# Sparse attention and a gated expert layer: the largest of v by TensorE, stores from ScalarE, a fifth softmax buffer, the gate's product kept in PSUM, the threshold on ScalarE

## The chip, the core and the metric

The kernel runs on one core of one Trainium2 chip. The metric is the device time of one execution in microseconds, the lower the better. One execution of the kernel before was also profiled: its trace gives start, length and engine of each instruction, and who released whom. The engines are TensorE (PE, with its weight loads shown as PEld), VectorE (DVE), ScalarE (ACT), GpSimd (POOL) and SyncE (SP, which before the change issues all DMAs).

## What is computed

Eight batches of eight heads, 576 queries and keys, 64 columns a head; then a layer of 512 to 2048 to 512 over the 4608 rows.

```python
scores = (1/8) * q @ k.T
thresh = scores.max(-1) - tau                 # tau = 0.02
attn = exp(where(scores >= thresh, scores, -1e9) - max)
attn = attn / (attn.sum(-1) + 1e-9)
x = concat_heads(attn @ v)                    # 4608 x 512
h = x @ w_in                                  # 4608 x 2048
out = (h * sigmoid(h)) @ w_out                # 4608 x 512
```

## The kernel before

Everything is held to nearly float32 precision by splitting operands into a high and a low float16 part, so that a product is three matmuls (high by high, high by low, low by high). The parts need a common scale, a power of two from the largest magnitude.

**Attention.** A *tile* is 128 queries of one head against all 576 keys; there are 288 tiles, and 36 for each batch from the second on (batch 0 is worked on in two rounds, whose first is in plain float32). The numbers in tile names count slots, some of which are empty, so that the last is 300. A tile goes through the engines like this: PE writes the scores into one of two PSUM buffers (L406); DVE takes the negated maximum (L416) and from it the threshold, maximum minus tau (L419, a 128x1 operation); ACT takes exp of the scores into an SBUF buffer w32 (L426), of which there are four in turn; DVE zeroes what is below the threshold and sums the rest (L435), which frees the scores' PSUM buffer, and takes the sum's reciprocal (L439, L443); ACT scales w32 (L448); POOL writes the high part (L459) and the two pieces of the low part (L462, L465) into a buffer hl, and with that last read w32 is free again; SP issues the DMA that transposes hl into wT (L475). When a pair of heads is complete, PE multiplies wT with the parts of v (L490), and ACT and DVE split the result into the high and the low part of x (L508, L509).

**v.** For each batch the four pieces of v are loaded (L227), DVE takes the largest magnitude of each in every partition (L233) and of the four (L110), and POOL's custom instruction partition_all_reduce takes the largest over the partitions (L113). Six small DVE operations make scales of it (L116 to L131), and then ACT and DVE split v (L270, L271).

**Experts.** A group of 256, 320 or 288 columns is worked on in units: 16 units of h, one for each 128 rows of d_ff, with 12 matmuls (L524), then 16 quarters of o with 12 matmuls each (L562), four to each output block. h and o take the same PSUM banks in turn: three (m0 to m2) from the middle of batch 0 on, two before that. After a unit of h come four operations: ACT takes tanh of h/2 into a buffer th in SBUF, of which there are two (L532); DVE makes (tanh + 1) * h and writes it back into th (L533), the last read of the bank; ACT writes its high part, times 2^-14, into gbuf (L541; the first four of the run are written by POOL, L543); DVE writes the low part (L547). After the fourth quarter of o, ACT scales the bank into one of two buffers ot (L571) and SP issues the store (L573).

**Order.** Python emits all this slot by slot, one tile and some units of the experts in each, with a pace that spreads the units of a group over the tiles until the next one; a scheduler then orders the instructions of each engine by priority and by its own idea of time, and adds the waits. Each engine, and SP's queue of DMAs, runs its instructions strictly in that order. When attention is done, the experts of the last groups are left. The two decoders of the weights at the start (L173 to L206) share the engines with batch 0.

Of the kernel before, what the change touches and what calls it, by code (L numbers as in the profile page):

```python
# [28 lines left out]
GB = 17  # buffers of g: a group of 16 and one ahead  # L29
WSPARE = 2  # raw weights lie this far ahead of the split ones, which take their place  # L30
LOAD = 5  # tiles that the loads of q and k run ahead
AV_LAG = 3  # tiles from a visit's last to its product with v
EARLY = 36  # tiles in which ACT still rounds the weights of attention for GpSimd
GAP, GAP1 = 12, 1  # free slots before batch 0's second visits and before batch 1
V_SLOT = 26  # batch 0's values are split from here on
RATES = (1.3, 0.8)  # units of the experts per slot while batch 0's two groups are there
RATE = 0.95
# weights: first chunk, slots of the decoding and of the splitting, priority
# [3 lines left out]
# a visit of two heads: its tiles of 128 queries (4: the last 64 of both heads) for the  # L42
# first and the second head, and the query ranges that it completes
# [8 lines left out]
def attention_moe(  # L52
# [21 lines left out]
    # three banks in turn; the last one is for the sums of the weights while they come in  # L74
# [7 lines left out]
    # ---------------------------------------------------------------- constants  # L82
    tau_sb = const.tile([P, 1], F32, name="tau_sb")
    nc.sync.dma_start(out=tau_sb, in_=tau)
    # 1/8 where the threshold can be met (tau >= 0), else 0: all scores equal, all kept
# [9 lines left out]
    # stacks of (hi; lo) rows of q, with 64 zero columns for the shared tile  # L95
# [9 lines left out]
    def pow2_scales(mx, name, across=True):  # L105
        """From mx [P, n] (bounds >= 0, per partition or, without across, the same on all):
        s = 2^(13-e) and 1/s for the largest's exponent e."""
# [3 lines left out]
        if across:  # L111
            allp = const.tile([P, 1], F32, name=f"{name}_all", tag=f"{k}_all")
            nc.gpsimd.partition_all_reduce(allp, one, P, bass.bass_isa.ReduceOp.max)  # L113
            one = allp
# [21 lines left out]
    # ---------------------------------------------------------------- weights  # L136
# [29 lines left out]
    def decode_weights(i):  # L166
        """float64 words to float32: the sign, 8 bits of the exponent (2^-112 on the top word
        read as float32 takes the exponent's bias down), 23 of the fraction."""
# [15 lines left out]
        # sums of the magnitudes over the rows of four chunks, four columns at a time: they  # L184
        # bound h (w_in), w_out
# [33 lines left out]
    # ---------------------------------------------------------------- values  # L219
# [56 lines left out]
    # ---------------------------------------------------------------- q and k  # L276
# [12 lines left out]
    def qcol(h, i):  # L289
        """Column of query tile i in the stack (even: 0..3, last, zeros; odd: zeros, last,  # L290
        2, 3, 0, 1)."""
        return i * P if h % 2 == 0 else (0, 384, 512, 128, 256)[(i + 1) % 5]
# [30 lines left out]
    # the first visits work in float32 throughout: the tensor engine has time for them  # L323
# [53 lines left out]
    # ---------------------------------------------------------------- scores  # L377
    # a tile: (visit, [(head, query tile, first row, rows)])
# [32 lines left out]
    def soft1(t):  # L411
        s_ps = sps[t]
        sm = sb.tile([P, 5], F32, tag="small", name=f"sm_{t}", bufs=4)
        w = sb.tile([P, S], F32, tag="w32", name=f"w32_{t}", bufs=4)
        negm, thr = sm[:, 0:1], sm[:, 1:2]
        nc.vector.tensor_reduce(  # L416
            out=negm, in_=s_ps[:, :, :HALF], op=ALU.max, axis=AX.XY, negate=True
        )
        nc.vector.tensor_scalar(  # L419
# [5 lines left out]
    def soft1b(t):  # L425
        nc.scalar.activation(  # L426
            wtile[t].rearrange("p (j c) -> p j c", j=2), sps[t][:, :, :HALF], AF.Exp,
            bias=small[t][:, 0:1],
        )
# [351 lines left out]
```

## Time and profile before

| | |
|---|---|
| runs | median 1358.73 us, 1357.87 to 1359.26 (3 runs) |
| profiled execution, span from its first to its last instruction | 1360.4 us |
| last instruction of POOL's work on attention | about 1236 us |
| mean granted clock of PE over the span | 0.950 |
| stores: size and time from issue to landing | 56 of 144 KB, 2.0 us |
| transposing DMAs (L475) | 304, 3.3 us |
| instructions that load a table of functions on ACT | 1, of 1.3 us |

The span of the profiled execution is what the profile has for its own time; it lies 1.7 us above the median of the runs. Rows of groups read: line, engine, operation, result<-operands, partitions x elements, count | busy us, mean ns of one | idle time of the engine before them, and what ended most of it. In a timeline the brackets at the end of a row give that idle time and its releaser for one instruction; "issue" stands for a wait that the profile does not explain. Rows of waits read: who waited <- for whom: us in total, times, longest.

### The profile page before, as it was taken

What the parts mean: (1) busy time and instruction counts of PE and PEld (TensorE: products, weight loads), DVE (VectorE), ACT (ScalarE), POOL (GpSimd) and SP (SyncE); (2) the same over time, 40 slices, a digit from 0 to 9 for tenths busy, and PEclk for the clock granted to TensorE, in tenths of its full rate; (3) what the DMA queues carried; (4) which work ended last, traced back from release to release, by engine and by line L of the source; (5) the groups of instructions that cost most, each with busy time, mean ns of one, the idle gap of its engine ahead of it and who ended that gap; (6) DMA issues with size and microseconds to landing.
All of it is one profiled execution on the core that took longest, in us unless ns stands there. A gap on an engine that the chain in (4) does not pass through costs nothing.

```text
span 1360.4 us, 26858 instructions
## 1 busy us (share of the span) xinstructions
PE 1183.7 (87%) x9392; PEld 899.9 (66%) x9392; DVE 1002.8 (74%) x2619; ACT 817.5 (60%) x1493; POOL 789.9 (58%) x964
## 2 busy tenths in 40 slices
PE   3774787898599979898899969899799999999998
PEld 2453555666477757676677757677577777777777
DVE  4987997897598967968497856869478787872421
ACT  3776775675476756656375745757367666662432
POOL 2647984787478656754476646556467666661000
PEclk9887888999799999999899979999799999999999
DMA  6454955778467656664475556565466565543000
GB/s 226 140 185 125 197 129 94 146 139 170 88 133 155 122 106 129 131 128 86 99 132 124 118 96 136 101 127 121 82 122 116 115 129 115 106 88 53 6 19 18
DMA packets 363479, 158.15 MB, mean 116 GB/s; under 512 B 329552, under 2 KB 338256, under 8 KB 363344
## 3 DMA queue, kind: packets, MB, share of 16 engines
q1 hardware_dynamic: 363344, 156.43, 55.5%
q8 instruction: 74, 1.21, 0.4%
q14 instruction: 61, 0.50, 0.1%
HBM read 66.72 MB, written 9.44 MB: 56 GB/s over the span
## 4 chain that ended last, share of the span: by engine, by line
DVE 35%; PE 34%; issue 13%; ACT 6%; POOL 6%; DMA 5%; SPq 2%; POOLq 0%; ACTq 0%; DVEq 0%
PE o L562 15%; PE h L524 8%; DVE w L435 8%; DVE sm L416 6%; DVE gbuf L547 6%; PE s L406 5%; PE a L490 5%; DVE qstack L310 3%; DVE th L533 3%; DMA vraw<-in_vL 2%; DMA wT<-hl 2%; ACT w L426 2%; POOL hl L459 2%; POOL hl L462 2%; ACT w L448 2%
## 5 line engine op out<-in xcount | busy, mean ns | idle before, releaser
L524 PE MATMUL h<-x,wst 128*128 128x288 f16 (+2 forms) x3072 | 422.3, 290 | 22.6 <-DVE th L533 19.1
L562 PE MATMUL o<-gbuf,wst 128*128 128x288 f16 (+2 forms) x3072 | 419.4, 293 | 22.4 <-DVE gbuf L547 16.1
L562 PEld LDWEIGHTS <-wst 128*128 128x128 f16 x3072 | 296.4, 100 | 117.1 <-issue 27.1
L459 POOL TENSOR_SCALAR hl<-w 128x576 f16<-128x576 f32 x264 | 187.3, 710 | 317.9 <-ACT w L448 69.1
L524 PEld LDWEIGHTS <-wst 128*128 128x128 f16 x3072 | 290.7, 99 | 119.2 <-issue 37.5
L462 POOL TENSOR_TENSOR hl<-w,hl 128x512 f16<-128x512 f32 x272 | 332.0, 1220 | 28.0 <-issue 13.9
L426 ACT ACTIVATE w<-s,sm 128x576 f32<-128x576 f32 x288 | 211.0, 736 | 204.5 <-POOL hl L465 135.4
L435 DVE SCALAR_TENSOR_TENSOR w<-s,sm,w 128x576 f32<-128x576 f32 x288 | 232.6, 810 | 110.4 <-ACT w L426 108.7
L448 ACT ACTIVATE w<-w,sm 128x576 f32<-128x576 f32 x288 | 218.2, 770 | 86.5 <-DVE sm L443 81.6
L416 DVE TENSOR_REDUCE sm<-s 128x1 f32<-128x576 f32 x288 | 215.1, 748 | 44.4 <-PE s L406 42.3
L406 PE MATMUL s<-khi,qstack 128*128 128x288 f32 x608 | 160.4, 346 | 70.0 <-DVE w L435 36.9
L547 DVE SCALAR_TENSOR_TENSOR gbuf<-th,gbuf 128x288 f16<-128x288 f32 (+2 forms) x256 | 167.3, 656 | 20.9 <-ACT gbuf L541 20.2
L406 PEld LDWEIGHTS s<-khi,qstack 128*128 128x128 f32 x608 | 98.5, 198 | 98.8 <-issue 71.4
L490 PE MATMUL a<-wT,v 128*64 128x288 f16 (+1 forms) x1680 | 142.4, 294 | 16.1 <-DMA wT<-hl 15.0
L532 ACT ACTIVATE th<-h,msc 128x288 f32<-128x288 f32 (+2 forms) x256 | 126.3, 495 | 49.5 <-DVE gbuf L547 30.0
L541 ACT ACTIVATE gbuf<-th 128x288 f16<-128x288 f32 (+2 forms) x252 | 109.9, 438 | 44.5 <-DVE th L533 43.9
L406 PE MATMUL s<-klo,qstack 128*128 128x288 f32 x608 | 134.2, 304 | 0.0
L533 DVE SCALAR_TENSOR_TENSOR th<-th,h 128x288 f32<-128x288 f32 (+2 forms) x256 | 113.2, 444 | 27.6 <-ACT th L532 25.4
L490 PEld LDWEIGHTS <-v 128*64 128x64 f16 x1680 | 91.3, 110 | 56.7 <-issue 41.9
L465 POOL TENSOR_TENSOR hl<-w,hl 128x64 f16<-128x64 f32 x272 | 115.3, 424 | 0.0
L406 PEld LDWEIGHTS s<-klo,qstack 128*128 128x128 f32 x608 | 102.2, 197 | 0.0
L320 POOL TENSOR_TENSOR klo<-kraw,khi 128x576 fp32r<-128x576 f32 x64 | 95.6, 1493 | 1.4 <-ACT khi L318 1.3
(82 smaller groups left out, 868.8 us busy)
## 6 DMA issues: line engine op xcount, KB each, us to landing
qraw<-in_qT SPq DMA_DIRECT2D x128, 144.0 KB, 3.0
kraw<-in_kT SPq DMA_DIRECT2D x128, 144.0 KB, 3.0
vraw<-in_vL SPq DMA_DIRECT2D x32, 320.0 KB, 3.5
wraw<-in_w_out SPq DMA_DIRECT2D x16, 512.0 KB, 4.0
out_t<-ot SPq DMA_DIRECT2D x56, 144.0 KB, 2.0
wT<-hl SPq DMA_TRANSPOSE x304, 3.3
gbuf<-in_w_in SPq DMA_DIRECT2D x8, 512.0 KB, 5.1
wraw<-in_w_in SPq DMA_DIRECT2D x8, 512.0 KB, 4.9
```

What stands on the lines that cost most here:

```text
L406: nc.tensor.matmul(s_ps[:, j, :HALF], lhs, kk[:, j * HALF : (j + 1) * HALF], start=(n == 0), stop=(n == len(seq) - 1),)
L416: nc.vector.tensor_reduce(out=negm, in_=s_ps[:, :, :HALF], op=ALU.max, axis=AX.XY, negate=True)
L426: nc.scalar.activation(wtile[t].rearrange("p (j c) -> p j c", j=2), sps[t][:, :, :HALF], AF.Exp, bias=small[t][:, 0:1],)
L435: nc.vector.scalar_tensor_tensor(out=w3, in0=s_ps[:, :, :HALF], scalar=sm[:, 1:2], in1=w3, op0=ALU.is_ge, op1=ALU.mult, accum_out=sm[:, 2:3],)
L448: nc.scalar.activation(w, w, AF.Copy, scale=r)
L459: nc.gpsimd.tensor_scalar(out=fl[:, 0:S], in0=w, scalar1=1.0, scalar2=1.0, op0=ALU.mult, op1=ALU.mult)
L462: nc.gpsimd.tensor_tensor(out=fl[:, 640:1152], in0=w[:, 0:512], in1=fl[:, 0:512], op=ALU.subtract)
L490: nc.tensor.matmul(a_ps[odd * D : (odd + 1) * D, :n], vt[:, lo_v, odd, kv, :], wT[v, b * H + 2 * p + odd][:, kw, c0 - base : c0 - base + n ...
L524: nc.tensor.matmul(ph[:, :n], wi(c, f, lo_w), x16[b, lo_x][:, c, c0 : c0 + n], start=(k == 0), stop=(k == 11),)
L533: nc.vector.scalar_tensor_tensor(out=th[:, :n], in0=th[:, :n], scalar=1.0, in1=ph[:, :n], op0=ALU.add, op1=ALU.mult,)
L547: nc.vector.scalar_tensor_tensor(out=g[:, 1, :n], in0=th[:, :n], scalar=2.0**-14, in1=g[:, 0, :n], op0=ALU.mult, op1=ALU.subtract,)
L562: nc.tensor.matmul(ps[:, :n], wo(f, d, lo_w), g[:, lo_g, :n], start=(f == 0 and k == 0), stop=(f == NF - 1 and k == 2),)
```

## The change

- **Largest of v.** L113 is gone. ACT scales the rows of the 128x128 identity by the per-partition maxima, in bfloat16 (new L115), PE multiplies a matrix of ones with this diagonal (L117), so that each partition holds all 128 maxima in one PSUM bank of the rotation, and DVE takes their maximum (L119).
- **Threshold.** L419 is gone from DVE; ACT computes it after exp as -1 * negm + ntau (L432).
- **Softmax buffers.** Five of w32 instead of four.
- **Gate.** (tanh + 1) * h is written back into the PSUM bank of h instead of th (L538, before L533); the high part (L545, now always ACT) and the low part (L546, before L547) read it there.
- **Stores.** The result o is scaled into two spare places of the weights' array instead of buffers of its own, and its store is issued by ACT instead of SP (L573).
- Comments are gone, which moves the line numbers by some lines: L406 is L411, L416 is L421, L426 is L428, L435 is L440, L448 is L453, L459, L462, L465 are L464, L467, L470, L524 is L529, L562 is L561.

```diff
         if across:
-            allp = const.tile([P, 1], F32, name=f"{name}_all", tag=f"{k}_all")
-            nc.gpsimd.partition_all_reduce(allp, one, P, bass.bass_isa.ReduceOp.max)
-            one = allp
+            diag = const.tile([P, P], BF16, name=f"{name}_diag", tag="diag")
+            nc.scalar.activation(diag, ident, AF.Copy, scale=one)
+            allp = bank([P, P], f"{name}_ps")
+            nc.tensor.matmul(allp, ones, diag, start=True, stop=True)
+            one = const.tile([P, 1], F32, name=f"{name}_all", tag=f"{k}_all")
+            nc.vector.tensor_reduce(out=one, in_=allp, op=ALU.max, axis=AX.X)
...
-        w = sb.tile([P, S], F32, tag="w32", name=f"w32_{t}", bufs=4)
+        w = sb.tile([P, S], F32, tag="w32", name=f"w32_{t}", bufs=5)
...
-        nc.vector.tensor_scalar(
-            out=thr, in0=negm, scalar1=-1.0, scalar2=ntau, op0=ALU.mult, op1=ALU.add
-        )
...
+        nc.scalar.activation(
+            small[t][:, 1:2], small[t][:, 0:1], AF.Identity, scale=-1.0, bias=ntau
+        )
...
             nc.vector.scalar_tensor_tensor(
-                out=th[:, :n], in0=th[:, :n], scalar=1.0, in1=ph[:, :n],
+                out=ph[:, :n], in0=th[:, :n], scalar=1.0, in1=ph[:, :n],
...
-            if gcount[0] > 4:
-                nc.scalar.activation(g[:, 0, :n], th[:, :n], AF.Copy, scale=2.0**-14)
-            else:
-                nc.gpsimd.tensor_scalar(
-                    out=g[:, 0, :n], in0=th[:, :n], scalar1=2.0**-14, scalar2=1.0,
-                    op0=ALU.mult, op1=ALU.mult,
-                )
+            nc.scalar.activation(g[:, 0, :n], ph[:, :n], AF.Copy, scale=2.0**-14)
             nc.vector.scalar_tensor_tensor(
-                out=g[:, 1, :n], in0=th[:, :n], scalar=2.0**-14, in1=g[:, 0, :n],
+                out=g[:, 1, :n], in0=ph[:, :n], scalar=2.0**-14, in1=g[:, 0, :n],
...
-            o = sb.tile([P, WID], F32, tag="o", name=f"ot_{b}_{c0}_{d}", bufs=2)
+            o = wst[:, NW + d % 2, :]
...
-            nc.sync.dma_start(out=outT[d * P : (d + 1) * P, c : c + n], in_=o[:, :n])
+            nc.scalar.dma_start(out=outT[d * P : (d + 1) * P, c : c + n], in_=o[:, :n])
```

The scheduler orders each engine anew. Three places show how.

POOL, before, at the all-reduce for batch 4, while it splits the weights of tiles 121 and 122 (ISA rows are custom instructions or what sets them up):

```order
L459 TENSOR_SCALAR hl_121_5756<-w32_121_5715 128x576
L462 TENSOR_TENSOR hl_121_5756<-w32_121_5715,hl_121_5756 128x512
L465 TENSOR_TENSOR hl_121_5756<-w32_121_5715,hl_121_5756 128x64
L113 ISA
L113 ISA v4_all_7711<-v4_one_7709 128x1
L459 ISA
L459 TENSOR_SCALAR hl_122_5808<-w32_122_5746 128x576
```

ACT, after, where the same batch's diagonal (v4_diag) is built, between the softmax of tiles 130 to 133 and the stores of batch 1's last group:

```order
L432 ACTIVATE sm_131_6256<-sm_131_6256,ntau_81 128x1
L573 DMA out_t<-wst_89 128x288
L571 ACTIVATE wst_89<-o_1_288_1_5687,msc_1_3622 128x288
L453 ACTIVATE w32_130_6202<-w32_130_6202,sm_130_6201 128x576
L573 DMA out_t<-wst_89 128x288
L428 ACTIVATE w32_132_6299<-s_132_6259,sm_132_6298 128x576
L432 ACTIVATE sm_132_6298<-sm_132_6298,ntau_81 128x1
L453 ACTIVATE w32_131_6257<-w32_131_6257,sm_131_6256 128x576
L115 ACTIVATE v4_diag_7707<-ident_93,v4_one_7705 128x128
```

PE, after, takes the matmul of this diagonal behind the scores of tile 164, among the matmuls of o:

```order
L411 MATMUL s_164_8123<-khi_33_7852,qstack1_87 128x288 x2
L411 MATMUL s_164_8123<-klo_33_7854,qstack1_87 128x288 x2
L561 LDWEIGHTS wst_89
L561 MATMUL o_2_288_0_7654<-gbuf_61,wst_89 128x288
```

```order
L117 LDWEIGHTS ones_91
L117 MATMUL v4_ps_7709<-v4_diag_7707,ones_91 128x128
L561 LDWEIGHTS wst_89
L561 MATMUL o_2_288_0_7654<-gbuf_61,wst_89 128x288
```

POOL has no custom instruction any more; the step is spread over ACT, PE and DVE, and the store's issue stands on ACT between the activations of softmax. The last place is DVE in batch 3's first group, from a unit's product with h (th_3_0_4, h_3_0_4) to its low part. Before:

```order
L533 SCALAR_TENSOR_TENSOR th_3_0_4_8321<-th_3_0_4_8321,h_3_0_4_8274 128x288
L435 SCALAR_TENSOR_TENSOR w32_172_8676,sm_172_8675<-s_172_8638,sm_172_8675,w32_172_8676 128x576
L419 TENSOR_SCALAR sm_173_8734<-sm_173_8734,ntau_81 128x1
L439 TENSOR_SCALAR sm_172_8675<-sm_172_8675 128x1
L533 SCALAR_TENSOR_TENSOR th_3_0_5_8363<-th_3_0_5_8363,h_3_0_5_8308 128x288
L435 SCALAR_TENSOR_TENSOR w32_173_8735,sm_173_8734<-s_173_8679,sm_173_8734,w32_173_8735 128x576
L443 RECIPROCAL sm_172_8675<-sm_172_8675 128x1
L547 SCALAR_TENSOR_TENSOR gbuf_61<-th_3_0_4_8321,gbuf_61 128x288
```

And after:

```order
L538 SCALAR_TENSOR_TENSOR h_3_0_4_8270<-th_3_0_4_8317,h_3_0_4_8270 128x288
L440 SCALAR_TENSOR_TENSOR w32_173_8731,sm_173_8730<-s_173_8674,sm_173_8730,w32_173_8731 128x576
L444 TENSOR_SCALAR sm_173_8730<-sm_173_8730 128x1
L448 RECIPROCAL sm_173_8730<-sm_173_8730 128x1
L315 SCALAR_TENSOR_TENSOR qstack1_87<-qraw_22_37_8791,gate_79,qstack1_87 64x576
L440 SCALAR_TENSOR_TENSOR w32_174_8776,sm_174_8775<-s_174_8733,sm_174_8775,w32_174_8776 128x576
L546 SCALAR_TENSOR_TENSOR gbuf_61<-h_3_0_4_8270,gbuf_61 128x288
L538 SCALAR_TENSOR_TENSOR h_3_0_5_8304<-th_3_0_5_8359,h_3_0_5_8304 128x288
```

Between the two operations of one unit stand five others now and six before; before the second one the bank of h was already free, now it is not. On PE the 16 units of h of this group stand among the scores of tiles 170 to 182, before 169 to 178.

More of the change, by code (lines that the diff above doesn't have):

```diff
@@ L413, in soft1 @@
         sm = sb.tile([P, 5], F32, tag="small", name=f"sm_{t}", bufs=4)
-        w = sb.tile([P, S], F32, tag="w32", name=f"w32_{t}", bufs=4)
-        negm, thr = sm[:, 0:1], sm[:, 1:2]
+        w = sb.tile([P, S], F32, tag="w32", name=f"w32_{t}", bufs=5)
+        negm = sm[:, 0:1]
         nc.vector.tensor_reduce(
             out=negm, in_=s_ps[:, :, :HALF], op=ALU.max, axis=AX.XY, negate=True
-        )
-        nc.vector.tensor_scalar(
-            out=thr, in0=negm, scalar1=-1.0, scalar2=ntau, op0=ALU.mult, op1=ALU.add
         )
```

## Prediction

> **What bounds the kernel now.** I read the page first: the busy shares say that no engine is full over the whole span.
>
> ```profile
> PE 1183.7 (87%) x9392; PEld 899.9 (66%) x9392; DVE 1002.8 (74%) x2619; ACT 817.5 (60%) x1493; POOL 789.9 (58%) x964
> ```
>
> PE's 87% is an average over stages, so I took the stages apart. The time from 440 to 1235 us is a regular alternation: 16 units of h (an "h-stretch", 192 matmuls), then the 16 quarters of o that use them (an "o-stretch", also 192), with scores and products with v in between. I found their borders in PE's timeline and asked for busy time by window. First four o-stretches with nearly the same matmuls (columns: length, then busy time and count of each engine, granted clock, DMA), then in the same way two h-stretches.
>
> ```profile
> core 0: us, PE busy (x) PEld busy (x) DVE busy (x) ACT busy (x) POOL busy (x), PEclk, DMA share, GB/s
> ...
> 633.80:681.00 47.20, 37.75 (x288) 28.72 (x287) 23.31 (x71) 19.08 (x32) 22.14 (x30) 0.89 0.45 93
> 716.80:750.30 33.50, 33.49 (x288) 26.42 (x287) 23.38 (x64) 19.03 (x33) 21.12 (x27) 1.00 0.59 125
> 787.90:835.30 47.40, 36.30 (x287) 27.98 (x286) 23.95 (x71) 18.73 (x33) 21.67 (x30) 0.86 0.48 92
> 873.40:910.80 37.40, 33.94 (x288) 26.66 (x288) 27.11 (x66) 20.40 (x34) 22.11 (x29) 1.00 0.57 121
> 947.20:994.70 47.50, 38.23 (x287) 28.96 (x286) 23.15 (x71) 19.30 (x32) 21.63 (x30) 0.86 0.50 90
> 1030.50:1065.20 34.70, 33.80 (x289) 26.62 (x288) 23.79 (x63) 19.20 (x33) 21.20 (x27) 1.00 0.61 118
> ```
>
> ```profile
> 596.20:633.80 37.60, 34.79 (x293) 26.69 (x291) 34.47 (x88) 28.34 (x56) 24.73 (x32) 1.00 0.64 129
> ...
> 1065.20:1100.00 34.80, 34.80 (x291) 26.29 (x290) 31.93 (x87) 27.73 (x56) 24.83 (x31) 1.00 0.60 117
> ```
>
> Every second o-stretch takes 47.4 us, the one after it 33.5 to 37.4, for the same work on every engine. Without that excess the stretches are close to PE's own pace: a PE busy throughout took 34.8 us for an h-stretch, the usual one takes 37.6 with DVE at 34.5. What the long ones contain, POOL's, DVE's and ACT's timelines of the third show:
>
> ```profile
> 957.33 0.38 POOL L113 PARTITION_ALL_REDUCE v_all<-v_one  x1 [5.91 <-issue]
> 964.73 0.67 POOL L459 TENSOR_SCALAR hl<-w 128x576 f16<-128x576 f32 x1 [7.03 <-issue]
> ```
>
> ```profile
> 957.74 0.15 DVE L116 TENSOR_SCALAR v_cl<-v_all 128x1 f32<-128x1 f32 x1 [5.84 <-POOL v_all L113]
> ```
>
> ```profile
> 966.83 0.74 ACT L426 ACTIVATE w<-s,sm 128x576 f32<-128x576 f32 x1 [13.41 <-POOL hl L465]
> ```
>
> The all-reduce itself takes 0.38 us, but POOL does nothing for 5.9 us before and 7.0 us after it, waiting for nothing that the profile shows. DVE, in order, stands before v_cl meanwhile; ACT's exp then finds no free w32 buffer for 13.4 us, since POOL's last read of a tile (L465) frees it; with no exp there are no new scores, and PE, in order, stands before them. The list of waits and the tile's own answer give the totals:
>
> ```profile
> ACT w L426 <- POOL hl L465: 135.4, 54, 14.4
> ...
> POOL hl L459 <- issue: 67.5, 8, 11.1
> ...
> POOL v_all L113 <- issue: 43.9, 7, 7.5
> ...
> DVE v_cl L116 <- POOL v_all L113: 35.3, 8, 7.0
> ```
>
> ```profile
> L113 POOL PARTITION_ALL_REDUCE v_all<-v_one x8: 377/378/379, 19.1 to 957.3; - x8
> ```
>
> Eight such stops, one for each batch. Two other stages matter. From 120 to 200 us DVE is the bound, busy for 79.3 of the 80 us:
>
> ```profile
> 120.00:200.00 80.00, 57.88 (x397) 41.77 (x395) 79.32 (x175) 59.26 (x107) 72.87 (x75) 0.83 0.73 165
> ```
>
> And after 1235 us there is only PE's work on the last groups, 192 matmuls in 23.68 us, which no edit here shortens:
>
> ```profile
> 1309.42 23.68 PE L524 MATMUL h<-x,wst 128*128 128x288 f16 x192
> ```
>
> **The change, part by part.** (A) The largest of v. POOL's custom instruction goes; in its place stand one ACTIVATE of 128x128, one matmul and one DVE reduction of 128x128 for each batch. POOL is no longer in this path at all. The stop costs 47.4 - 35.2 = 12.2 us where I can compare (35.2 is the mean of 33.5, 37.4 and 34.7). I take 12 for each of the five of batches 3 to 7, and 10 for the three of batches 0 to 2, where a freed DVE soon meets its own limit: 5 x 12 + 3 x 10 = 90 us. Bounds: 35 (what DVE itself waits) and 8 x 12.2 = 98. The new instructions are cheap: some 8 x (0.3 + 0.3 + 0.7) = 10 us over three engines, at the prices of L362 (277 ns, below) and at most L416-like reductions, and they wait for little: the order above has the diagonal of batch 4 built on ACT among the softmax of tiles 130 to 133 and its matmul on PE behind the scores of tile 164, some 30 tiles later. What PE could wait for there is one bank of its rotation.
>
> (B) DVE's load. These rows, from the groups kept apart by shape, price what leaves DVE:
>
> ```profile
> L547 DVE SCALAR_TENSOR_TENSOR gbuf<-th,gbuf 128x288 f16<-128x288 f32 x224 | 144.9, 650 | 20.5 <-ACT gbuf L541 19.9
> ...
> L533 DVE SCALAR_TENSOR_TENSOR th<-th,h 128x288 f32<-128x288 f32 x224 | 99.4, 445 | 27.6 <-ACT th L532 25.4
> ...
> L419 DVE TENSOR_SCALAR sm<-sm,ntau 128x1 f32<-128x1 f32 x288 | 59.0, 207 | 2.8
> ...
> L509 DVE SCALAR_TENSOR_TENSOR x<-a,x 128x288 f16<-128x288 f32 x56 | 25.2, 449 | 43.9 <-ACT x L508 43.8
> ```
>
> The threshold takes 59.0 us of DVE. L547 reads th and gbuf, both in SBUF, at 650 ns; L509 is the same operation with its first operand in PSUM, at 449. After the change L547 has that form: 224 x 0.2 = 45 us less. That the 650 is not the form's own price shows in the groups of the tail, where POOL is idle:
>
> ```profile
> L547 DVE SCALAR_TENSOR_TENSOR gbuf<-th,gbuf 128x288 f16<-128x288 f32 x32 | 14.7, 458 | 15.4 <-ACT gbuf L541 15.3
> ```
>
> L533 now writes PSUM, which no DVE instruction of this trace does; its reading counterpart L509 costs no more than SBUF, so I keep 445 (bounds 400 to 510). Together 104 us of 1002.8, 10%. Of that, what lies on the path: 10% of the 79 us in which DVE is full, 8 us; and in eight h-stretches at most 37.6 - 34.8 = 2.8 us each, of which I take 1, another 8. So 16 us (0 to 30).
>
> [...]
>
> (C) The bank is held longer. Before, L533 freed the bank of h; now L546, the last of the four operations, does. I look at the gap in DVE's timeline for two units that were in flight together (two L533, then their two L547):
>
> ```profile
> 688.68 0.44 DVE L533 SCALAR_TENSOR_TENSOR th<-th,h 128x288 f32<-128x288 f32 x1
> ...
> 689.91 0.44 DVE L533 SCALAR_TENSOR_TENSOR th<-th,h 128x288 f32<-128x288 f32 x1
> ...
> 691.06 1.13 DVE L547 SCALAR_TENSOR_TENSOR gbuf<-th,gbuf 128x288 f16<-128x288 f32 x1
> ...
> 692.19 0.49 DVE L547 SCALAR_TENSOR_TENSOR gbuf<-th,gbuf 128x288 f16<-128x288 f32 x1
> ```
>
> The ends are 3.07 and 2.33 us apart, so a bank would be held some 2.7 us longer, in a rotation of three banks at 37.6 / 16 = 2.35 us per unit, 7.05 us per turn. Two rows of the waits say how tight both buffers are now:
>
> ```profile
> ACT th L532 <- DVE gbuf L547: 30.0, 34, 2.8
> ...
> PE h L524 <- DVE th L533: 19.1, 20, 2.8
> ```
>
> PE rarely waits for a bank, and th, of which there are two, is freed earlier by the change, so ACT's tanh can follow sooner. The order also spreads the 16 units over more tiles than before (h of batch 3's first group: tiles 170 to 182, before 169 to 178). I charge 10 us (0 to 40; beyond that it is a rival). In the tail the chain tanh, DVE, copy repeats on ACT every 1.47 us, exactly PE's pace (23.68 / 16 = 1.48):
>
> ```profile
> 1268.52 0.50 ACT L532 ACTIVATE th<-h,msc 128x288 f32<-128x288 f32 x1
> ...
> 1269.99 0.50 ACT L532 ACTIVATE th<-h,msc 128x288 f32<-128x288 f32 x1
> ```
>
> The copy gets 0.03 us shorter if it reads PSUM like L508 (405 against L541's 438 in the next fence), so I leave the tail alone.
>
> (D) What ACT gains in work. The rows:
>
> ```profile
> L541 ACT ACTIVATE gbuf<-th 128x288 f16<-128x288 f32 x224 | 97.7, 438 | 39.4 <-DVE th L533 39.0
> ...
> L571 ACT ACTIVATE ot<-o,msc 128x288 f32<-128x288 f32 x56 | 27.7, 494 | 63.9 <-PE o L562 63.7
> ...
> L508 ACT ACTIVATE x<-a 128x288 f16<-128x288 f32 x56 | 22.7, 405 | 40.9 <-PE a L490 40.8
> ...
> L362 ACT ACTIVATE wT<-tl 128x128 f32<-128x128 f32 x16 | 4.4, 277 | 0.0
> ```
>
> ACT has no 128x1 operation yet. From 405 at 288 elements and 277 at 128, 0.8 ns an element, one element would take 175 ns; a scale read from a tile costs 494 - 405 = 89 more, so 265 for the threshold with its bias (bounds 175 and 277): 288 x 0.265 = 76 us. A store's issue takes SP's queue 0.71 us, and its waits there are long:
>
> ```profile
> 657.41 0.71 SPq L573 DMA_DIRECT2D out_t<-ot  x1
> ```
>
> ```profile
> SPq L573 <- ACT ot L571: 160.0, 27, 30.9
> ```
>
> On ACT that is 64 x 0.7 = 45 us, and the next exp stands behind each. ACT is busy for 28 of 37.6 us in an h-stretch, where 11 or 12 thresholds add 3, and 19 of 35 in an o-stretch, where four stores and their waits add about 5. I count 0 (bounds +40 and -10). In return SP no longer stands 160 us before stores with transposes and loads behind them; the waits that this ends are partly the stops of (A), so 0 more. The fifth w32 buffer lets one more exp run ahead of POOL; of the 135.4 us above most goes with (A), so 0 (to -10).
>
> Sum against the profiled span: 1360.4 - 90 - 16 + 10 = 1264.4. That span lies 1.7 us above the median of the runs, 1358.73, so 1263.
>
> **The rivals.** (1) PSUM banks become the bound, and the kernel is slower. If PE waits for a bank at every turn, each unit of h takes up to 2.7 / 3 = 0.9 us longer; 14 of the 16 groups lie outside the tail, 224 units, up to 202 us. It decides once more than 106 / 224 = 0.47 us per unit shows; at 0.55 the time is 1358.7 - 106 + 123 = 1376. For it: five other instructions of DVE lie between L538 and L546 in the order. Against it: the 19.1 us above, and the th buffers. [...] Chance 8%.
>
> (2) ACT becomes the late one: a store at the head of its queue waits for its activation and for an earlier DMA, and exp, which frees the scores, comes late. At the upper bound of (D) with 40 us, 1303; with less of the stops regained, up to 1340. For it: exp and the store now share a queue; against it: ACT's idle 9 to 16 us per stretch. Chance 19%.
>
> (3) With the stops gone, PE's pace holds everywhere: the whole 98 us of (A), 30 of (B), nothing for (C), and 10 from the fifth buffer: 1358.7 - 138 = 1221. For it: the stretches of 33.5 and 34.8 us. Against it: h-stretches keep DVE at 34. Chance 18%.
>
> That the stop simply stays is excluded by the order: POOL has no custom instruction any more.
>
> **How the numbers follow.** The forecast, 1240 to 1285, has 55%. The range 1222 to 1308 takes in most of rivals 2 and 3 and leaves out the first. A measurement of this kernel can tell 0.2% (2.7 us) from no change. Rivals 2, 3 and the forecast are all faster: 0.92. Of rival 1's 8%, 2 lie within 0.2% of 1358.73 and 6 above.
>
> **What would show it.** Right: no idle time of POOL of 6 or 7 us that the profile puts down to nothing; every o-stretch between 33 and 38 us; L546 near 450 ns; DVE busy near 900 us; a tail of the same 23.7 us per 192 matmuls. Wrong: PE waiting for L546 in tens of microseconds (rival 1); ACT's exp late behind the stores (rival 2); o-stretches still alternating, which would mean that the stop was not POOL's.

## The result and the profile after

| | before | after |
|---|---|---|
| median of the runs, us | 1358.99 (1357.87 to 1360.19, 4 runs) | 1277.77 (1274.11 to 1282.37, 4 runs) |
| ratio | | 0.9395, 95% interval 0.9368 to 0.9421 |
| span of the profiled execution, us | 1360.4 | 1275.1 |
| from the first instruction to the third group of h | 333.4 | 313.7 |
| from there to the fourteenth group of h (the *main stage*) | 869.4 | 804.4 |
| from there to the end | 157.6 | 157.0 |

The kernel is 81 us faster by the medians and 85.3 by the two profiled executions; the forecast was 96. The split into three stages goes by PE's first matmul of a group of h (groups of 16 units and 16 quarters, 16 of them), so that the same h and o lie in a stage in every kernel here; of attention's matmuls a few more or fewer do, and with the stores on SP 75 more than in the changed kernel lie in the first stage and 75 fewer in the main one. Of the 85.3 us, 19.7 come before the third group, 65.0 in the main stage, and 0.6 in the end. One of the six runs of the changed kernel in a later round was slow, 1373.32 us at a clock of 0.831 where the other five had 0.960 to 0.969, and is left out of its median below.

The first line of the page after shows what became of the engines.

```profile
PE 1174.1 (92%) x9400; PEld 895.7 (70%) x9400; DVE 930.6 (73%) x2339; ACT 866.9 (68%) x1793; POOL 759.8 (60%) x952
```

DVE lost 72 us of work (1002.8 before), ACT gained 49 (817.5 before). Neither tells where the time went; the two stages do, first of before, then of after (length, then busy time and count of each engine, granted clock, DMA).

```profile
0.00:333.40 333.40, 244.98 (x1658) 173.68 (x1659) 277.82 (x687) 219.30 (x390) 227.44 (x258) 0.89 0.65 154
333.40:1202.80 869.40, 784.86 (x6450) 605.21 (x6448) 667.32 (x1796) 538.27 (x979) 541.65 (x679) 0.96 0.59 117
```

```profile
0.00:313.70 313.70, 242.00 (x1669) 176.10 (x1670) 275.63 (x626) 237.72 (x476) 226.53 (x257) 0.88 0.72 168
313.70:1118.10 804.40, 778.53 (x6455) 599.57 (x6453) 601.85 (x1586) 570.62 (x1189) 512.61 (x666) 0.99 0.64 124
```

In the main stage PE stood idle for 869.4 - 784.9 = 84.5 us before and for 804.4 - 778.5 = 25.9 after, at nearly the same count of matmuls. PE is now busy for 97% of the main stage. That is the new bound, and it leaves 26 us for anything else to win or lose on there without making PE's own work shorter.

The stretches changed their form. These are two groups of the main stage after the change, an h-stretch, an o-stretch, and the same again:

```profile
474.40:519.00 44.60, 41.30 (x351) 30.87 (x349) 38.52 (x108) 36.01 (x79) 34.48 (x48) 1.00 0.77 149
519.00:546.70 27.70, 27.70 (x230) 22.29 (x230) 12.94 (x30) 13.07 (x25) 10.89 (x13) 1.00 0.44 98
546.70:586.20 39.50, 38.60 (x326) 28.93 (x323) 31.91 (x88) 32.32 (x72) 25.60 (x37) 1.00 0.63 114
586.20:617.30 31.10, 30.36 (x255) 24.21 (x254) 23.78 (x53) 18.41 (x36) 18.75 (x23) 1.00 0.59 134
```

The new order puts more scores beside h (351 and 326 matmuls where it was some 291) and fewer beside o (230 and 255 against 288). So the forecast's "every o-stretch between 33 and 38 us" is not what the trace shows, but 28 and 31 in these two; the 47 us stretches are gone all the same, and the clock no longer falls to 0.86 in them.

The waits now, over the whole span, and from the groups the instructions that the forecast priced:

```profile
POOL klo L325 <- ACT khi L323: 115.2, 14, 16.2
...
ACT w L428 <- POOL hl L470: 71.0, 40, 5.2
...
POOL hl L464 <- issue: 43.1, 5, 15.6
...
DVE w L440 <- ACT sm L432: 30.7, 50, 1.4
...
PE s L411 <- DVE w L440: 20.8, 26, 2.2
...
PE h L529 <- DVE gbuf L546: 14.9, 13, 4.0
```

```profile
L546 DVE SCALAR_TENSOR_TENSOR gbuf<-h,gbuf 128x288 f16<-128x288 f32 x224 | 100.6, 451 | 22.7 <-ACT gbuf L545 21.9
...
L538 DVE SCALAR_TENSOR_TENSOR h<-th,h 128x288 f32<-128x288 f32 x224 | 101.9, 456 | 42.4 <-ACT th L537 39.5
...
L432 ACT ACTIVATE sm<-sm,ntau 128x1 f32<-128x1 f32 x288 | 83.9, 292 | 5.5 <-DVE sm L421 5.3
...
L115 ACT ACTIVATE v_diag<-ident,v_one 128x128 bf16<-128x128 f32 x8 | 3.1, 392 | 6.1 <-DVE v_one L110 6.1
...
L119 DVE TENSOR_REDUCE v_all<-v_ps 128x1 f32<-128x128 f32 x8 | 2.2, 278 | 0.0
...
L117 PE MATMUL v_ps<-v_diag,ones 128*128 128x128 bf16 x8 | 1.7, 219 | 0.3 <-ACT wT L366 0.3
```

The largest of v now takes 0.39 us of ACT, 0.22 of PE and 0.28 of DVE for each batch, and no engine in the list waits for a result of ACT's or PE's part; ACT itself stands 6.1 us before the first of the eight. PE's wait for the bank of h went from 19.1 to 14.9 us although the bank is held longer. POOL still has long idle times, so a gap on POOL alone is no sign of the old stop. The longest, with what PE did meanwhile:

```profile
467.08 1.41 POOL L325 TENSOR_TENSOR klo<-kraw,khi 128x576 fp32r<-128x576 f32 x1 [16.23 <-ACT khi L323]
```

```profile
466.31 0.69 ACT L323 ACTIVATE khi<-kraw 128x576 fp32r<-128x576 f32 x1 [0.23 <-PE s L411]
```

```profile
446.00:467.00 21.00, 21.00 (x170) 17.12 (x170) 17.32 (x43) 14.39 (x29) 4.85 (x7) 1.00 0.37 94
```

POOL stands for 16.23 us in this window, and PE is busy for all 21.00 of it. POOL waits for ACT to round the next keys (khi), and ACT starts on them when PE's scores let it: POOL now waits for PE, where before PE waited because POOL did.

### The profile page after: what moved, and what is told of

The parts are those of the page before. It is cut to its first block, busy times and chain, and to the rows that moved or that the text cites. A ratio compares the mean times of both kernels' runs of the same rounds, so it can differ in the third digit from the quotient of the medians.

```text
span 1275.1 us, 26912 instructions
## 1 busy us (share of the span) xinstructions
PE 1174.1 (92%) x9400; PEld 895.7 (70%) x9400; DVE 930.6 (73%) x2339; ACT 866.9 (68%) x1793; POOL 759.8 (60%) x952
## 4 chain that ended last, share of the span: by engine, by line
PE 52%; DVE 19%; DMA 9%; issue 7%; POOL 6%; ACT 5%; SPq 1%; ACTq 0%; POOLq 0%; DVEq 0%
PE o L561 20%; PE h L529 16%; PE s L411 8%; DMA wT<-hl 7%; PE a L495 6%; DVE w L440 4%; DVE sm L421 3%; POOL hl L467 2%; POOL hl L464 2%; DMA vraw<-in_vL 2%; DVE wst L211 2%; DVE v L276 1%; DVE h L538 1%; DVE wst L185 1%; ACT w L453 1%
## 5 line engine op out<-in xcount | busy, mean ns | idle before, releaser
L529 PE MATMUL h<-x,wst 128*128 128x288 f16 (+2 forms) x3072 | 425.1, 292 | 19.1 <-DVE gbuf L546 14.9
L561 PE MATMUL o<-gbuf,wst 128*128 128x288 f16 (+2 forms) x3072 | 396.5, 286 | 0.0
L529 PEld LDWEIGHTS <-wst 128*128 128x128 f16 x3072 | 291.7, 100 | 117.3 <-issue 33.1
L561 PEld LDWEIGHTS <-wst 128*128 128x128 f16 x3072 | 291.8, 98 | 81.4 <-issue 4.7
L467 POOL TENSOR_TENSOR hl<-w,hl 128x512 f16<-128x512 f32 x272 | 328.5, 1208 | 12.5
L464 POOL TENSOR_SCALAR hl<-w 128x576 f16<-128x576 f32 x264 | 184.9, 701 | 215.3 <-DMA wT<-hl 76.2
L440 DVE SCALAR_TENSOR_TENSOR w<-s,sm,w 128x576 f32<-128x576 f32 x288 | 232.8, 812 | 94.7 <-ACT w L428 60.6
L428 ACT ACTIVATE w<-s,sm 128x576 f32<-128x576 f32 x288 | 213.1, 740 | 111.8 <-POOL hl L470 71.0
L421 DVE TENSOR_REDUCE sm<-s 128x1 f32<-128x576 f32 x288 | 215.9, 751 | 73.2 <-PE s L411 66.8
L453 ACT ACTIVATE w<-w,sm 128x576 f32<-128x576 f32 x288 | 218.8, 772 | 71.8 <-DVE sm L448 67.1
L411 PE MATMUL s<-khi,qstack 128*128 128x288 f32 x608 | 158.8, 343 | 21.0 <-DVE w L440 20.8
L495 PE MATMUL a<-wT,v 128*64 128x288 f16 (+1 forms) x1680 | 147.4, 294 | 11.4 <-DMA wT<-hl 9.8
L538 DVE SCALAR_TENSOR_TENSOR h<-th,h 128x288 f32<-128x288 f32 (+2 forms) x256 | 116.2, 455 | 43.1 <-ACT th L537 40.1
L411 PE MATMUL s<-klo,qstack 128*128 128x288 f32 x608 | 132.7, 301 | 0.0
L546 DVE SCALAR_TENSOR_TENSOR gbuf<-h,gbuf 128x288 f16<-128x288 f32 (+2 forms) x256 | 114.9, 450 | 23.6 <-ACT gbuf L545 22.6
L411 PEld LDWEIGHTS s<-khi,qstack 128*128 128x128 f32 x608 | 97.4, 196 | 48.2 <-issue 26.9
L545 ACT ACTIVATE gbuf<-h 128x288 f16<-128x288 f32 (+2 forms) x256 | 104.3, 408 | 37.7 <-DVE h L538 36.0
L411 PEld LDWEIGHTS s<-klo,qstack 128*128 128x128 f32 x608 | 100.6, 195 | 0.0
L470 POOL TENSOR_TENSOR hl<-w,hl 128x64 f16<-128x64 f32 x272 | 99.7, 366 | 0.0
```

Of the source, the lines that this page charges most:

```text
L411: nc.tensor.matmul(s_ps[:, j, :HALF], lhs, kk[:, j * HALF : (j + 1) * HALF], start=(n == 0), stop=(n == len(seq) - 1),)
L421: nc.vector.tensor_reduce(out=negm, in_=s_ps[:, :, :HALF], op=ALU.max, axis=AX.XY, negate=True)
L428: nc.scalar.activation(wtile[t].rearrange("p (j c) -> p j c", j=2), sps[t][:, :, :HALF], AF.Exp, bias=small[t][:, 0:1],)
L440: nc.vector.scalar_tensor_tensor(out=w3, in0=s_ps[:, :, :HALF], scalar=sm[:, 1:2], in1=w3, op0=ALU.is_ge, op1=ALU.mult, accum_out=sm[:, 2:3],)
L453: nc.scalar.activation(w, w, AF.Copy, scale=r)
L464: nc.gpsimd.tensor_scalar(out=fl[:, 0:S], in0=w, scalar1=1.0, scalar2=1.0, op0=ALU.mult, op1=ALU.mult)
```

## The experiments

All in one table; *first* and *main* are the two stages above, from each kernel's profiled execution. The ratio is to the kernel before, run on the same chip.

| kernel | median, us | ratio (95%) | first | main |
|---|---|---|---|---|
| largest of v alone | 1281.91 | 0.9389 (0.935 to 0.9428) | 312.1 | 806.1 |
| all but the largest of v | 1370.33 | 1.0047 (1.0024 to 1.007) | 353.3 | 857.1 |
| before, two calls a batch | 1423.22 | 1.0428 (1.0387 to 1.0469) | 368.4 | 893.6 |
| after, four softmax buffers | 1294.28 | 0.9477 (0.9427 to 0.9528) | 313.1 | 821.2 |
| after, once more | 1277.10 | 0.9403 (0.9374 to 0.9432) | 311.5 | 804.4 |
| after, gate in SBUF | 1278.96 | 0.9414 (0.9386 to 0.9442) | 307.9 | 813.3 |
| after, stores on SP | 1288.69 | 0.9474 (0.9449 to 0.9499) | 322.1 | 808.3 |
| after, threshold on DVE | 1276.93 | 0.9384 (0.9359 to 0.941) | 309.4 | 802.0 |
| after, threshold on DVE, four buffers | 1278.52 | 0.9379 (0.9355 to 0.9403) | 302.3 | 812.2 |
| largest of v, stores on ACT, five buffers | 1291.65 | 0.9495 (0.9475 to 0.9516) | 312.5 | 824.3 |
| largest of v, stores on ACT | 1290.44 | 0.9484 (0.946 to 0.9509) | 310.6 | 819.9 |
| largest of v for batches 3 to 7 alone | 1303.68 | 0.9579 (0.9559 to 0.9599) | 337.4 | 805.3 |

Theory: POOL's eight stops were the loss, and nearly all of the gain is their removal. Rivals: the gain needs DVE's relief too; the stores, thresholds and banks cost or bring something of their own.

**The largest of v alone.** The kernel before, with only this:

```diff
-            allp = const.tile([P, 1], F32, name=f"{name}_all", tag=f"{k}_all")
-            nc.gpsimd.partition_all_reduce(allp, one, P, bass.bass_isa.ReduceOp.max)
-            one = allp
+            diag = const.tile([P, P], BF16, name=f"{name}_diag", tag="diag")
+            nc.scalar.activation(diag, ident, AF.Copy, scale=one)
+            allp = bank([P, P], f"{name}_ps")
+            nc.tensor.matmul(allp, ones, diag, start=True, stop=True)
+            one = const.tile([P, 1], F32, name=f"{name}_all", tag=f"{k}_all")
+            nc.vector.tensor_reduce(out=one, in_=allp, op=ALU.max, axis=AX.X)
```

> The kernel before with only the largest of v moved from POOL's custom instruction to ACT, PE and DVE. Theory (POOL's eight stops were the loss, the rest of the change is worth little): 1265 to 1290 us, no idle time of POOL of 6 or 7 us that nothing explains. Rival (the stops hide a second bound, DVE with 34.5 of 37.6 us in the stretches of h, and the DVE relief of the other parts is needed to get the gain): 1305 to 1330 us.

1281.91 us: the whole gain of the change, as far as these runs can tell, comes with this one part, and DVE still does its old work. The second sign of the theory failed: POOL has six idle times, 60.8 us in all and up to 13.0, that the profile puts down to nothing, though no custom instruction is left. Its windows, the two stages and four o-stretches (groups 6 to 9; two of them were 47.2 and 47.4 us before):

```profile
0.00:312.10 312.10, 239.09 (x1661) 171.79 (x1662) 283.06 (x689) 221.10 (x394) 224.84 (x252) 0.90 0.71 165
312.10:1118.20 806.10, 769.49 (x6453) 598.84 (x6452) 660.49 (x1802) 537.59 (x982) 550.71 (x677) 0.99 0.65 125
590.50:624.80 34.30, 31.95 (x277) 25.33 (x276) 26.52 (x71) 19.66 (x33) 20.75 (x26) 1.00 0.66 140
662.60:695.80 33.20, 32.90 (x283) 25.82 (x282) 21.48 (x59) 17.19 (x29) 20.26 (x26) 1.00 0.57 120
730.40:765.90 35.50, 33.58 (x292) 26.88 (x290) 27.17 (x77) 20.64 (x35) 24.33 (x29) 1.00 0.69 150
803.90:838.70 34.80, 33.23 (x283) 25.86 (x282) 22.81 (x59) 18.01 (x32) 20.70 (x26) 1.00 0.59 116
```

Here the rest keeps nearly its old order (277 to 292 matmuls a stretch), and these stretches are what the forecast said: 33 to 36 us, no alternation. The rival (1305 to 1330 us) falls: with DVE at 660.5 us in the main stage it takes 806.1, with DVE at 601.9 (the whole change) 804.4.

**All but the largest of v.** The reverse: the changed kernel with POOL's instruction back.

> The changed kernel with POOL's custom instruction put back: all the rest of the change without its first part. Theory: the eight stops come back at 10 to 12 us each, 1345 to 1365 us. Rival (the fifth softmax buffer, the freed DVE and the stores off SP's queue let the other engines run through a stop): 1300 to 1325 us, with stretches of o that no longer alternate by more than 6 us.

1370.33 us, a little above the theory's range and slower than the kernel before by 0.2 to 0.7%. The other four parts bring nothing in sum while the stops are there: neither the fifth buffer nor the freed DVE carries the kernel through a stop. The main stage is 12 us shorter than before, the first 20 us longer; why the first, no run here settles.

**Two calls.** What is a stop? In the kernel before:

```diff
             nc.gpsimd.partition_all_reduce(allp, one, P, bass.bass_isa.ReduceOp.max)
-            one = allp
+            allq = const.tile([P, 1], F32, name=f"{name}_alq", tag=f"{k}_alq")
+            nc.gpsimd.partition_all_reduce(allq, allp, P, bass.bass_isa.ReduceOp.max)
+            one = allq
```

> The kernel before with POOL's custom instruction issued twice in a row for each batch (the second on the result of the first, which it leaves as it is). Theory (POOL stands still because something has to be brought in when it turns from its ordinary instructions to this one and back): the second call costs 0.4 to 1 us, 1358 to 1368 us in all. Rival (each call brings its own 6 us before and 7 us after): a second stop of up to 13 us for each of eight batches, 1420 to 1465 us.

1423.22 us, 61 more: the low end of the rival's range, and far outside the theory's. Yet the trace shows neither a second stop for each call nor a cheap second call throughout, since the order put the two calls next to each other in four batches and apart in the other four. POOL's timeline around a pair of each sort (L113 is the first call, L115 the second) shows the difference:

```profile
366.12 0.31 POOL L467 TENSOR_TENSOR hl<-w,hl 128x64 f16<-128x64 f32 x1
372.36 0.38 POOL L113 PARTITION_ALL_REDUCE v_all<-v_one  x1 [5.94 <-issue]
372.84 0.35 POOL L115 PARTITION_ALL_REDUCE v_alq<-v_all  x1
380.63 0.67 POOL L461 TENSOR_SCALAR hl<-w 128x576 f16<-128x576 f32 x1 [7.44 <-issue]
```

```profile
109.77 0.38 POOL L113 PARTITION_ALL_REDUCE v_all<-v_one  x1 [5.92 <-issue]
117.12 0.64 POOL L175 TENSOR_SCALAR wst<-wraw 128x512 f32<-128x512 f32 x1 [6.98 <-issue]
123.76 0.38 POOL L115 PARTITION_ALL_REDUCE v_alq<-v_all  x1 [6.00 <-issue]
130.90 1.39 POOL L322 TENSOR_TENSOR klo<-kraw,khi 128x576 fp32r<-128x576 f32 x1 [6.76 <-issue]
```

Next to each other the second call costs 0.1 + 0.35 us; one ordinary instruction between them, and both turns are paid again, 6.0 us to the custom instruction and 6.8 back. So the stop belongs to the turn, not to the call: the theory had the turn right and the total wrong, because half of the pairs were split, and the rival had the total by luck. Four more stops for 61 us is 15 us each. That something is brought in at a turn, as the theory says, no run shows. At the eight stops of the kernel before, POOL stands 5.8 to 7.5 us on the way in and 6.7 to 7.4 us on the way back: both are paid at every stop, not only at the first.

**The first three stops.** The largest of v goes to TensorE for batches 3 to 7 alone:

```diff
+LATE = ("v3", "v4", "v5", "v6", "v7")
...
+            if name in LATE:
+                diag = const.tile([P, P], BF16, name=f"{name}_diag", tag="diag")
...
+            else:
+                allp = const.tile([P, 1], F32, name=f"{name}_all", tag=f"{k}_all")
+                nc.gpsimd.partition_all_reduce(allp, one, P, bass.bass_isa.ReduceOp.max)
+                one = allp
```

> The kernel before with the largest of v moved to ACT, PE and DVE for batches 3 to 7 alone; the first three batches keep POOL's custom instruction and its stops. Theory (by the lead of one kernel over the other at PE's groups, the first three stops cost some 7 us each and the other five 12.6): 1294 to 1302 us. Rival (all stops cost about 10 us each): 1306 to 1316 us.

1303.68 us lies between the two ranges; the stages decide.

```profile
0.00:337.40 337.40, 245.36 (x1657) 175.30 (x1658) 278.09 (x687) 219.66 (x390) 227.45 (x257) 0.87 0.64 152
337.40:1142.70 805.30, 768.91 (x6454) 597.37 (x6452) 663.82 (x1801) 536.87 (x984) 549.61 (x675) 0.99 0.65 126
```

The main stage, whose five stops are gone, takes 805.3 us, 64.1 less than before: 12.8 a stop. The first stage keeps its three stops and is 25.3 us longer than with the largest of v moved for all batches (312.1): 8.4 a stop, or 7.1 if that kernel is held against before (333.4).

**The changed kernel once more**, as the measure for the three that undo one part each on the same chip.

> The changed kernel once more, on the same chip as the three that undo one part each: 1274 to 1282 us by either theory.

1277.10 us, with the same 804.4 us of the main stage.

**The gate in SBUF.** In the changed kernel:

```diff
-                out=ph[:, :n], in0=th[:, :n], scalar=1.0, in1=ph[:, :n],
+                out=th[:, :n], in0=th[:, :n], scalar=1.0, in1=ph[:, :n],
...
-            nc.scalar.activation(g[:, 0, :n], ph[:, :n], AF.Copy, scale=2.0**-14)
+            nc.scalar.activation(g[:, 0, :n], th[:, :n], AF.Copy, scale=2.0**-14)
...
-                out=g[:, 1, :n], in0=ph[:, :n], scalar=2.0**-14, in1=g[:, 0, :n],
+                out=g[:, 1, :n], in0=th[:, :n], scalar=2.0**-14, in1=g[:, 0, :n],
```

> The changed kernel with the product (tanh + 1) * h written back into th in SBUF, as before. Theory (the bank is held longer, which costs about what the shorter low-part instruction of DVE brings): within 8 us of the changed kernel, the low part on DVE back near 650 ns. Rival 1 (banks held longer cost): 5 to 20 us faster, PE no longer waiting for a bank. Rival 2 (DVE's relief is on the path): 8 to 25 us slower.

1278.96 against 1277.10 us on the same chip: no difference that can be told, though in the profiled executions the main stage is 8.9 us longer and the first 3.6 shorter. The low part is back at its old price, and PE's wait for the bank is half of after's:

```profile
L546 DVE SCALAR_TENSOR_TENSOR gbuf<-th,gbuf 128x288 f16<-128x288 f32 x224 | 148.3, 665 | 26.3 <-ACT gbuf L545 25.7
```

```profile
PE h L529 <- DVE th L538: 7.5, 9, 1.5
```

DVE does 48 us more in the first and the main stage (925.8 against 877.5), PE waits 7.4 us less for banks, and the time stays. This run alone can't tell two prices of nothing from two that cancel, which is what the theory expected. The next experiment, which gives DVE work back and leaves the banks as they are (ACT gets less to do), and the largest of v alone, with all of DVE's old work, are no slower either. Together the three speak for DVE's relief not being on the path. The low part took 665 ns here, the mean of the whole run with both operands in SBUF, against 451 with one operand in PSUM (the changed kernel), and 458 with both in SBUF in the tail of before, where POOL is idle; whether POOL's work makes that difference was not tried by itself.

**The threshold, and the fifth buffer.** Three kernels: the changed one with the threshold back on DVE (its lines moved back), with `bufs=4` for w32, and with both.

> The changed kernel with the threshold back on DVE, where it took 207 ns against ACT's 286. Theory (neither engine bounds the stretches any more): within 6 us. Rival 1 (DVE is the bound before 200 us and in the stretches of h): 8 to 25 us slower. Rival 2 (ACT's exp comes late behind the thresholds): 6 to 20 us faster.

> The changed kernel with four softmax buffers instead of five. Theory (the fifth buffer was there to ride out POOL's stops, and PE's own pace bounds the kernel now): within 5 us of the changed kernel's 1277.8 us. Rival (exp's wait for a buffer, still 71.0 us in the changed kernel's trace, is on the path): 1288 to 1305 us.

> The changed kernel with the threshold back on DVE and four softmax buffers. Theory (the threshold behind exp on ACT keeps the masking on DVE waiting, so each softmax buffer is taken for longer, and the fifth buffer pays for that): 1274 to 1284 us, the 16 us that four buffers cost the changed kernel are gone. Rival (the fifth buffer is needed whatever computes the threshold): 1288 to 1298 us.

1276.93, 1294.28 and 1278.52 us. The threshold alone makes no difference that can be told; with ACT's threshold four buffers cost 10 us (by the ratios) to 17 (by the medians), with DVE's threshold nothing. So the theory that the fifth buffer was for POOL's stops falls. It pays for the threshold on ACT, after whose exp the masking on DVE has one more instruction to wait for: DVE's wait for L432 is 30.7 us in the changed kernel, and with DVE's threshold there is none. The scores' bank is freed by that masking. PE's wait for it, and exp's wait for a softmax buffer, which the rival on record named, with four buffers and ACT's threshold, then with DVE's:

```profile
ACT w L428 <- POOL hl L470: 90.3, 44, 5.4
...
PE s L411 <- DVE w L440: 46.4, 33, 4.0
```

```profile
ACT w L431 <- POOL hl L470: 64.6, 33, 5.7
...
PE s L411 <- DVE w L440: 29.7, 24, 5.1
```

PE's rows differ by 16.7 us, exp's by 25.7, the two kernels by 10.8 in the first stage and 9.0 in the main one. That the buffer and the threshold belong together is shown; through which of the two waits it runs is not, as both fall together.

**The stores.** The changed kernel with its stores issued by SP (`nc.sync` for `nc.scalar` at L573), and, as their mirror, the largest of v with the stores on ACT from the spare places, once with four and once with five buffers:

> The changed kernel with the stores of the result issued by SP again, from the same two places. Theory (with the stops gone, the stores wait for little on either queue): within 6 us of the changed kernel. Rival 1 (the stores delay exp on ACT): 6 to 25 us faster. Rival 2 (transposes and loads wait behind the stores on SP): 6 to 30 us slower.

> The kernel before with the largest of v on TensorE and the stores issued by ACT from the two spare places; gate in SBUF, threshold on DVE, four buffers. Theory (stores off SP's queue bring what the changed kernel lost with them on SP, some 10 us): 1268 to 1275 us. Rival (the 10 us belong to the changed kernel's order of work alone, as the largest of v alone had its stores on SP and took 1281.9 us): 1277 to 1285 us.

> The changed kernel with the threshold back on DVE and the gate's product back in SBUF; what is left of the change is the largest of v, the stores on ACT and the fifth buffer. Theory (neither DVE's load nor the banks bound the kernel): within 6 us of the changed kernel's 1278 us. Rival 1 (DVE, with all its old work, becomes the bound): 1284 to 1300 us. Rival 2 (the two parts undone cost more than they bring): 1262 to 1271 us, faster than both kernels.

In the changed kernel the stores are worth 11.6 us on ACT (1288.69 against 1277.10; 10 by the ratios), in the range of the rival by which SP's transposes and loads wait behind them. SP does stand before its stores again (before: 160.0 us), but that this is what costs the time was not tried by itself:

```profile
SPq L573 <- ACT wst L571: 155.1, 25, 31.0
```

With the gate in SBUF and the threshold on DVE, stores on ACT come out slower: 1290.44 and 1291.65 us, where the largest of v alone took 1281.91. These two kernels also scale the result into the spare places, which the largest of v alone doesn't, and no run changes that by itself. With four buffers the expected 1268 to 1275 us were wrong, and so were the rival's 1277 to 1285; with five, the theory's 6 us around 1278. They lose it in the main stage, here with four and with five buffers:

```profile
310.60:1130.50 819.90, 778.36 (x6455) 601.43 (x6453) 665.56 (x1805) 539.33 (x985) 550.53 (x675) 0.99 0.64 124
```

```profile
312.50:1136.80 824.30, 783.03 (x6463) 601.14 (x6461) 671.49 (x1811) 545.01 (x983) 539.71 (x674) 0.99 0.64 123
```

Against the largest of v alone (806.1, PE busy 769.5) PE's idle time grows only from 36.6 to 41.5 and 41.3 us, and PE's busy time by 9 to 14 us for the same matmuls. The second time lies where the rival of a full DVE had it, but DVE is busy for 81% of the stage here and for 82% there, so the same work of DVE goes with the shorter stage too. What sets these 14 to 18 us is left open. What is shown is that the four small parts don't add up: stores on ACT bring 10 to 12 us in the changed kernel and go with 9 to 13 us more beside the largest of v alone, and the fifth buffer brings 10 to 17 us or nothing. All nine kernels with the full first part, the changed one among them, lie between 0.938 and 0.950. That the parts' prices change because each lets the scheduler order everything anew is likely and not shown. The two lowest, with the threshold on DVE, are not told apart from the changed kernel.

## Why the prediction was right, and where it was not

**What bound the kernel** was right: the stop of POOL, passed on through the softmax buffer and the scores to PE. Its removal alone gives the full gain, and its return takes it all back.

**(A)** The five stops of batches 3 to 7 were priced at 12 us each; the main stage gained 63.3 with this part alone, and 64.1 in the kernel that moves only these: 12.7 to 12.8 a stop. (The prediction announces four o-stretches for the price of a stop and shows six, three long and three short.) The three earlier ones were priced at 10, because a freed DVE would meet its limit. They gave 21.3 (25.3 by the other comparison): less than the five later ones, as forecast, and 5 to 9 us less than the sum had. The reason given, DVE's limit, fits and was not tried by itself: in the first stage DVE is busy for 283.1 of 312.1 us (91%) in the kernel with the largest of v alone, against 277.8 of 333.4 (83%) before.

**(B) and (C)** are the step that failed: -16 for a lighter DVE and +10 for the banks. Both prices per instruction were right (L546 took 451 ns for 449 forecast, L538 456 for 445), and both came to nothing on the path. "Of that, what lies on the path" was worked out from before, where PE idled 84.5 us of the main stage; with the stops gone it idles 26 to 37, and neither 65 us less of DVE's work there nor 4 us less of waiting for banks moved the end. The forecast's -6 for the two together, with (D) at nothing, is -0.4 in the spans (1275.5 for the largest of v alone against 1275.1). Each run that undoes one part moves several prices at once, so that some of them cancel can't be ruled out.

**(D)** came to nothing, as counted, but not for its reasons, and that was luck: undoing the stores or the buffer in the changed kernel costs some 10 us or more each. The threshold took 292 ns instead of 265, above the bound of 277. A store's issue took 0.34 us on ACT, as the median of 64; the 0.71 us on SP was one row, and the median there is 0.51, so the forecast's 45 us on ACT are 22:

```profile
526.75 0.34 ACTq L573 DMA_DIRECT2D out_t<-wst  x1
```

The fifth buffer was counted at nothing and does have a price, 10 to 17 us, but only against the threshold on ACT.

**The sum.** Forecast 96 us off the span, found 85.3. Of the 10.7 short, 8.7 are the first three stops, 5.6 are (B) with (C) and (D), and the five late stops gave 3.3 back (0.3 lies in the end). By the medians 4.1 more are missing, since the profiled execution of before was 1.4 above its median and that of after 2.7 below.

**The rivals.** Banks as the bound: PE's wait for them fell from 19.1 to 14.9 us. ACT as the late one: DVE's wait for exp fell from 108.7 to 60.6 us, exp's own (71.0 us, for POOL's last read) is half of before's, and with the stores off ACT the kernel is slower, not faster (1288.69 against 1277.10 us). PE's pace everywhere, 1221 us, had the right bound and the wrong time: it took PE's pace from the fastest stretches and added whole amounts of (A), (B) and the buffer, where PE's own busy time, 778.5 us, already leaves only 26 us of the main stage to gain.

**The signs** named: DVE busy near 900 us came out at 930.6, L546 at 451 ns, the tail unchanged:

```profile
1224.49 23.68 PE L529 MATMUL h<-x,wst 128*128 128x288 f16 x192
```

The sign "no idle time of POOL that nothing explains" was badly chosen: five such times, 43.1 us, remain, but without a custom instruction, and with PE busy for all of the 43.1 us. The o-stretches of 33 to 38 us came with the largest of v alone and not with the whole change.

## What to carry to other kernels

Look for an engine that stands idle with nothing to wait for, on both sides of one cheap instruction, and follow who stands behind it: the row of 0.38 us was worth 80 us. When several edits come together, price the rest against the idle time that the largest one leaves to the bounding engine (here 37 us of the main stage), not against what stands idle now. Here the price of a small edit changed with the other edits around it; undo each one by itself before believing its price, and mind what else the undoing moves.

## What the runs showed of the hardware

- POOL's stop lies in the turn between its ordinary instructions and the custom one: 5.8 to 7.5 us in and 6.7 to 7.4 us back at the eight stops of before. In the kernel with two calls a batch, two calls next to each other paid it once (5.94 us in, 0.1 between them, 7.44 back), two with an ordinary instruction between them twice (5.92 and 6.00 in, 6.98 and 6.76 back).
- In the long o-stretches of before, which hold the stops, PE's granted clock was 0.86 to 0.89 and some 288 matmuls kept PE busy for 36.3 to 38.2 us, against 33.5 to 33.9 for as many in the short ones, at a clock of 1.00. With the largest of v alone PE's busy time in the main stage was 769.5 us, at a clock of 0.99, against 784.9 at 0.96 before.
- The threshold, a 128x1 operation, took 292 ns on ACT as an activation with scale and bias (L432 of the changed kernel) and 207 on DVE (L419 of before).
- DVE's (tanh + 1) * h, 128x288, took 456 ns where it wrote its result to PSUM (L538 of the changed kernel) and 445 where it wrote it to SBUF (L533 of before).
